# One Strassen level in the down layer of a fused attention and MoE kernel, with one shared pool of four buffers for q, k and v

## Chip, cores, metric

The kernel runs on one core of one Trainium2 chip. The metric is device time in microseconds (us) of one execution. A profile's span is 1.7 to 1.9 us shorter than the time of the same execution. Engine names: PE is TensorE (PEld its weight loads), DVE is VectorE, ACT is ScalarE, POOL is GpSimd, SP is SyncE, which issues stores and transposing DMAs. The granted clock is the mean share of full speed at which PE was clocked. A DMA's landing time runs from its issue to the arrival of its last data.

## The reference, cut to what matters

```python
def _attn_ref(q, k, v, E, F):                     # 8 batches, 8 heads, 1024 tokens, 64 wide
    k_proj = np.einsum('ks,bhsd->bhkd', E, k)     # 1024 keys projected to 64
    v_proj = np.einsum('ks,bhsd->bhkd', F, v)
    scores = (1.0 / np.sqrt(q.shape[-1])) * np.matmul(q, k_proj.transpose(0, 1, 3, 2))
    ...                                           # softmax
    return np.matmul(attn, v_proj)

def _moe_ref(x, w1, w2, w_out):                   # x: 8192 tokens x 512; w1, w2: 512 x 1024
    g = np.maximum(x @ w1, x @ w2)
    return (g @ w_out).astype(np.float32)
```

The code is shortened and its comments are added. The kernel uses max(h1, h2) = relu(h1 - h2) + h2. So the up layer is x (w1 - w2) with a relu, and the down layer multiplies [relu, x] by [w_out, w2 w_out]: an inner dimension of 1024 + 512, or 12 blocks of 128.

## The kernel before

A batch has 1024 tokens in two halves j. In the up layer 8 slots a half run 4 matmuls of 512 columns, and DVE evacuates each bank (a tile of 128 x 512 fp32 in PSUM, into which PE accumulates) with a relu. In the down layer 4 output tiles a half accumulate 12 matmuls of 512 columns, and ACT copies them out. The attention of the next batch is strung between these slots: the projections (`step_kv`), the transpose of k (`step_kpt`), the scores (`step_sc`) and the rest (`step_da`), all in program order on each engine. From batch 2 on a DMA transposes q (`step_qt_dma`).

```python
    kvq = ctx.enter_context(tc.tile_pool(name="kvq", bufs=2))
    proj = ctx.enter_context(tc.tile_pool(name="proj", bufs=2))
    soft = ctx.enter_context(tc.tile_pool(name="soft", bufs=2))
    ...
    gpool = ctx.enter_context(tc.tile_pool(name="gpool", bufs=2))
    hpool = ctx.enter_context(tc.tile_pool(name="hpool", bufs=3))
    opool = ctx.enter_context(tc.tile_pool(name="opool", bufs=4))

    ...

    def mm_bank(dtype=FP32):
        return ps.tile(
            [128, 512 if dtype == FP32 else 1024], dtype, tag="mm", bufs=4, name="mm_ps"
        )

    def att_banks():
        return ps.tile([128, 2, 512], FP32, tag="att", bufs=2, name="att_ps")

    ...

    def alloc_kvq():
        t = {}
        for n in ("k", "v", "q"):
            t[n] = kvq.tile([128, H, NC, D], FP16, tag=n, name=f"{n}_sb")
        return t

    def load(t, n, src, b, h0, h1, c0=0, c1=NC):
        nc.gpsimd.dma_start(
            out=t[n][:, h0:h1, c0:c1, :],
            in_=src[b, h0:h1].rearrange("h (p c) d -> p h c d", c=NC)[:, :, c0:c1, :],
        )

    ...

    def step_qt_dma(t):
        nc.sync.dma_start_transpose(
            out=t["qt"].rearrange("q h (i p) -> q (h i) p", p=128),
            in_=t["q"].rearrange("p h c d -> p (h c d)"),
        )

    ...

    def step_sc(t, p):
        sc_ps = att_banks()
        for o in range(2):
            for e in range(2):
                pos = D * (o ^ e)
                nc.tensor.matmul(
                    out=sc_ps[pos : pos + KP, e, :],
                    lhsT=t["kpt"][o * D : (o + 1) * D, 2 * p + e, :],
                    rhs=t["qt"][o * D : (o + 1) * D, 2 * p + e, :],
                    start=True, stop=True,
                )
        ex = stage.tile([128, 2, HALF], FP16, tag="ex", name="ex_sb")
        t["ex"][p] = ex
        nc.scalar.activation(out=ex, in_=sc_ps, func=ACTF.Exp, scale=scale)

    def step_da(t, p):
        ex = t["ex"].pop(p)
        dn_ps = att_banks()
        at_ps = att_banks()
        for dst, w in ((dn_ps, None), (at_ps, t["vp"])):
            for r in range(2):
                for e in range(2):
                    o = r ^ e
                    rows = slice(r * KP, (r + 1) * KP)
                    nc.tensor.matmul(
                        out=dst[e * D : (e + 1) * D, o, :],
                        lhsT=ones16[rows, 0:D] if w is None else w[rows, 2 * p + e, :],
                        rhs=ex[rows, e, :],
                        start=True, stop=True,
                    )
        ld = soft.tile([128, 2, HALF], FP32, tag="ld", name="ld_sb")
        rec = soft.tile([128, 2, HALF], FP32, tag="rec", name="rec_sb")
        nc.scalar.activation(out=ld, in_=dn_ps, func=ACTF.Ln)
        nc.scalar.activation(out=rec, in_=ld, func=ACTF.Exp, scale=-1.0)

        def finish():
            nc.vector.tensor_tensor(
                out=t["xt"][:, p, :, :], in0=at_ps, in1=rec, op=ALU.mult
            )

        return finish

    ...

    def up_slots(t, j):
        t["gt", j] = gt = gpool.tile([128, NFB, HALF], FP16, tag="gt", name="gt_sb")
        for fb in range(NFB):
            def up(fb=fb):
                h_ps = mm_bank()
                for r in range(NDC):
                    nc.tensor.matmul(
                        out=h_ps,
                        lhsT=wd_sb[:, r, fb * 128 : (fb + 1) * 128],
                        rhs=t["xt"][:, r, :, j * W : (j + 1) * W],
                        start=(r == 0), stop=(r == NDC - 1),
                    )
                nc.vector.tensor_scalar_max(gt[:, fb, :], h_ps, 0.0)
            yield up

    def down_slots(b, t, j):
        for n2 in range(NI):
            o, i = n2 % 2, 2 * j + n2 // 2
            cell = {}
            g0 = (o * 2 + n2 // 2) * 128
            for part in range(3):
                def down(o=o, i=i, g0=g0, cell=cell, part=part):
                    gt = t["gt", j]
                    if part == 0:
                        cell["ps"] = mm_bank()
                    op_ps = cell["ps"]
                    for n in range(4 * part, 4 * part + 4):
                        if n < NFB:
                            lhsT, rhs = gt[:, n, g0 : g0 + 128], wo_sb[:, n, :]
                        else:
                            lhsT = t["xt"][:, n - NFB, o, i * 128 : (i + 1) * 128]
                            rhs = m_sb[:, n - NFB, :]
                        nc.tensor.matmul(
                            out=op_ps, lhsT=lhsT, rhs=rhs,
                            start=(n == 0), stop=(n == NFB + NDC - 1),
                        )
                    if part < 2:
                        return
                    o_sb = opool.tile([128, DM], FP32, tag="o", name="o_sb")
                    nc.scalar.copy(out=o_sb, in_=op_ps)
                    nc.sync.dma_start(
                        out=out.rearrange("(n p c) m -> n p c m", p=128, c=NC)[
                            b, :, 2 * i + o, :
                        ],
                        in_=o_sb,
                    )
                yield down

    ...

    core = {
        7: (step_kv,), 9: (step_kpt,), 13: (step_sc, 0),
        17: (step_da, 0), 19: (step_sc, 1), 23: (step_da, 1), 25: (step_sc, 2),
        29: (step_da, 2), 31: (step_sc, 3), 35: (step_da, 3),
    }
    late = {
        23: (step_kv,), 24: (step_kpt,), 25: (step_qt, 0), 27: (step_qt, 2), 28: (step_sc, 0),
        31: (step_da, 0), 32: (step_qt, 4), 33: (step_sc, 1), 36: (step_da, 1),
        37: (step_qt, 6), 38: (step_sc, 2), 41: (step_da, 2), 43: (step_sc, 3), 45: (step_da, 3),
    }
    by_dma = {1: (step_qt_dma,)}

    for b in range(B):
        nxt = None
        steps = {}
        if b + 1 < B:
            nxt = tiles[b + 1] = alloc_kvq()
            for n, src in (("k", k), ("v", v), ("q", q)):
                load(nxt, n, src, b + 1, 0, H)
            new_attn(nxt)
            steps = {n: [(s[0], nxt, *s[1:])] for n, s in (
                {**core, **by_dma} if b else late).items()}
    ...
```

The softmax here doesn't subtract the row's maximum and nothing guards it: scores larger than these inputs give would overflow.

Of the kernel before, what the change touches and what calls it, by code (L numbers as in the profile page):

```python
# [8 lines left out]
FP32 = mybir.dt.float32  # L9
FP16 = mybir.dt.float16  # L10
LN_EXP_SET = 6
ACTF = mybir.ActivationFunctionType
ALU = mybir.AluOpType
# [3 lines left out]
def kernel(  # L17
# [12 lines left out]
    nc = tc.nc  # L30

    B, H, S, D = q.shape
    KP = E.shape[0]
# [3 lines left out]
    NI = NC // 2  # L37
# [5 lines left out]
    scale = 1.0 / float(D) ** 0.5  # L43

    const = ctx.enter_context(tc.tile_pool(name="const", bufs=1))
    kvq = ctx.enter_context(tc.tile_pool(name="kvq", bufs=2))
    proj = ctx.enter_context(tc.tile_pool(name="proj", bufs=2))
    soft = ctx.enter_context(tc.tile_pool(name="soft", bufs=2))
    qtp = ctx.enter_context(tc.tile_pool(name="qtp", bufs=2))
    stage = ctx.enter_context(tc.tile_pool(name="stage", bufs=4))  # L50
    xpool = ctx.enter_context(tc.tile_pool(name="xpool", bufs=2))
    gpool = ctx.enter_context(tc.tile_pool(name="gpool", bufs=2))
    hpool = ctx.enter_context(tc.tile_pool(name="hpool", bufs=3))
    opool = ctx.enter_context(tc.tile_pool(name="opool", bufs=4))
    ps = ctx.enter_context(tc.tile_pool(name="ps", bufs=1, space=bass.MemoryType.PSUM))

    def mm_bank(dtype=FP32):
        return ps.tile(
            [128, 512 if dtype == FP32 else 1024], dtype, tag="mm", bufs=4, name="mm_ps"
        )  # L60

    def att_banks():
        return ps.tile([128, 2, 512], FP32, tag="att", bufs=2, name="att_ps")
# [12 lines left out]
    )  # L76


    ef_sb = const.tile([KP, 2, S], FP32)
    nc.sync.dma_start(out=ef_sb[:, 0, :], in_=E)  # L80
    nc.sync.dma_start(out=ef_sb[:, 1, :], in_=F)

    def alloc_kvq():
        t = {}
        for n in ("k", "v", "q"):
            t[n] = kvq.tile([128, H, NC, D], FP16, tag=n, name=f"{n}_sb")
        return t

    def load(t, n, src, b, h0, h1, c0=0, c1=NC):
        nc.gpsimd.dma_start(  # L90
# [1 line left out]
            in_=src[b, h0:h1].rearrange("h (p c) d -> p h c d", c=NC)[:, :, c0:c1, :],  # L92
        )

    tiles = {0: alloc_kvq()}
    for h0 in (0, H // 2):
        load(tiles[0], "k", k, 0, h0, h0 + H // 2)
        load(tiles[0], "q", q, 0, h0, h0 + H // 2, 0, NC // 2)
# [3 lines left out]
    load(tiles[0], "v", v, 0, 0, H // 2)  # L102
    load(tiles[0], "v", v, 0, H // 2, H)

    w1_sb = const.tile([128, NDC, DF], FP16)
    w2_sb = const.tile([128, NDC, DF], FP16)
    wo_sb = const.tile([128, NFB, DM], FP16)
    for f0 in range(0, DF, 256):
        if f0 == 256:
# [40 lines left out]
    def new_attn(t):  # L150
        t["kp"] = proj.tile([KP, H, D], FP16, tag="kp", name="kp_sb")
        t["vp"] = proj.tile([128, H, D], FP16, tag="vp", name="vp_sb")
        t["kpt"] = proj.tile([128, H, KP], FP16, tag="kpt", name="kpt_sb")
        t["xt"] = xpool.tile([128, NP2, 2, HALF], FP16, tag="xt", name="xt_sb")
        t["qt"] = qtp.tile([128, H, HALF], FP16, tag="qt", name="qt_sb")
        t["ex"] = {}


    def step_kv(t, h0=0, h1=H, which="kv"):
        kv_ps = mm_bank()  # L160
        n = (h1 - h0) * D
        both = which == "v"
        for c in range(NC):
            for w in which:
                i = "kv".index(w)
                for r in range(2) if both else (i,):
                    nc.tensor.matmul(  # L167
                        out=kv_ps[r * KP : (r + 1) * KP, 0:n],
                        lhsT=eft[:, i, c, :],
                        rhs=t[w][:, h0:h1, c, :],  # L170
                        start=(c == 0), stop=(c == NC - 1),
                    )
        fl = lambda ap: ap[:, h0:h1, :].rearrange("p h d -> p (h d)")
        if "k" in which:
            eng = nc.vector.tensor_copy if which == "k" else nc.scalar.copy
            eng(out=fl(t["kp"]), in_=kv_ps[0:KP, 0:n])  # L176
        if both:
            nc.vector.tensor_copy(out=fl(t["vp"]), in_=kv_ps[:, 0:n])
        elif "v" in which:
            nc.vector.tensor_copy(out=fl(t["vp"][KP:128]), in_=kv_ps[KP:128, 0:n])  # L180
            nc.vector.tensor_copy(out=fl(t["vp"][0:KP]), in_=kv_ps[KP:128, 0:n])


    def step_kpt(t, h0=0, h1=H):
        kpt_ps = mm_bank(FP16)
        for h in range(h0, h1):
            for r in range(2):
                nc.tensor.transpose(  # L188
                    out=kpt_ps[r * D : (r + 1) * D, (h - h0) * KP : (h - h0 + 1) * KP],
                    in_=t["kp"][:, h, :],  # L190
                    identity=ident16[:KP, :KP],
                )
        nc.vector.tensor_copy(
            out=t["kpt"][:, h0:h1, :].rearrange("q h k -> q (h k)"),
            in_=kpt_ps[:, 0 : (h1 - h0) * KP],
        )
# [26 lines left out]
    def step_sc(t, p):  # L223
# [11 lines left out]
        t["ex"][p] = ex  # L235
        nc.scalar.activation(out=ex, in_=sc_ps, func=ACTF.Exp, scale=scale)  # L236

    def step_da(t, p):
        ex = t["ex"].pop(p)
        dn_ps = att_banks()  # L240
        at_ps = att_banks()
# [9 lines left out]
                        start=True, stop=True,  # L251
                    )
        ld = soft.tile([128, 2, HALF], FP32, tag="ld", name="ld_sb")
        rec = soft.tile([128, 2, HALF], FP32, tag="rec", name="rec_sb")
        nc.scalar.activation(out=ld, in_=dn_ps, func=ACTF.Ln)  # L255
        nc.scalar.activation(out=rec, in_=ld, func=ACTF.Exp, scale=-1.0)  # L256

        def finish():
            nc.vector.tensor_tensor(  # L259
# [27 lines left out]
    def two_dn(t, g):  # L287
# [8 lines left out]
                    start=True, stop=True,  # L296
                )
        ld = soft.tile([128, 2, HALF], FP32, tag="ld", name="ld_sb")
        rec = soft.tile([128, 2, HALF], FP32, tag="rec", name="rec_sb")
        nc.scalar.activation(out=ld, in_=dn_ps, func=ACTF.Ln)  # L300
        nc.scalar.activation(out=rec, in_=ld, func=ACTF.Exp, scale=-1.0)
        t["rec", g] = rec

    def two_at(t, g, j):
# [22 lines left out]

    wd_sb = const.tile([128, NDC, DF], FP16)
    m_sb = const.tile([128, NDC, DM], FP16)
    w2t_sb = const.tile([128, NFB, DM], FP16)  # L330


    def up_slots(t, j):
        t["gt", j] = gt = gpool.tile([128, NFB, HALF], FP16, tag="gt", name="gt_sb")
        for fb in range(NFB):
            def up(fb=fb):
                h_ps = mm_bank()
                for r in range(NDC):
                    nc.tensor.matmul(  # L339
                        out=h_ps,  # L340
# [1 line left out]
                        rhs=t["xt"][:, r, :, j * W : (j + 1) * W],  # L342
                        start=(r == 0), stop=(r == NDC - 1),
                    )
                nc.vector.tensor_scalar_max(gt[:, fb, :], h_ps, 0.0)  # L345
            yield up

    def down_slots(b, t, j):
# [53 lines left out]
    def step_m(r):  # L402
# [6 lines left out]
        nc.scalar.copy(out=m_sb[:, r, :], in_=m_ps)  # L409


    t = tiles[0]
    new_attn(t)
    step_kv(t, 0, 4, "k")
    warm(2)
    step_kpt(t, 0, 4)
# [19 lines left out]
    warm(6)  # L436


    core = {
        7: (step_kv,), 9: (step_kpt,), 13: (step_sc, 0),  # L440
        17: (step_da, 0), 19: (step_sc, 1), 23: (step_da, 1), 25: (step_sc, 2),
        29: (step_da, 2), 31: (step_sc, 3), 35: (step_da, 3),
    }
    late = {
        23: (step_kv,), 24: (step_kpt,), 25: (step_qt, 0), 27: (step_qt, 2), 28: (step_sc, 0),
        31: (step_da, 0), 32: (step_qt, 4), 33: (step_sc, 1), 36: (step_da, 1),
        37: (step_qt, 6), 38: (step_sc, 2), 41: (step_da, 2), 43: (step_sc, 3), 45: (step_da, 3),
    }
    by_dma = {1: (step_qt_dma,)}

    for b in range(B):
        nxt = None
        steps = {}
        if b + 1 < B:
            nxt = tiles[b + 1] = alloc_kvq()
            for n, src in (("k", k), ("v", v), ("q", q)):
                load(nxt, n, src, b + 1, 0, H)
            new_attn(nxt)
            steps = {n: [(s[0], nxt, *s[1:])] for n, s in (
                {**core, **by_dma} if b else late).items()}  # L460
        t = tiles[b]
        if b == 0:
            u0, u1 = [*up_slots(t, 0)], [*up_slots(t, 1)]
            wt = [lambda f0=f0: step_w2t(f0) for f0 in range(0, DF, 256)]
            wd = [lambda f0=f0: step_wd(f0) for f0 in range(0, DF, 256)]
            f = lambda s, *a: lambda: s(t, *a)
            seq = [
                u0[0], u0[1], f(step_qt, 0, 4, NI // 2, NI), f(step_qt, 4, 4, NI // 2, NI), lambda: warm(2),
                f(two_sc, 0, 1), f(two_sc, 1, 1), wd[1], u0[2], f(two_dn, 0), u0[3],
                f(two_dn, 1), wd[2], f(two_at, 0, 1), u0[4], u0[5], wt[1], wd[3], f(two_at, 1, 1),  # L470
                wt[2], u0[6], wt[3], u0[7], *u1,
            ]
            base = len(seq) - 20
            seq += [lambda r=r: step_m(r) for r in range(NDC)]
            seq += [*down_slots(b, t, 0), *down_slots(b, t, 1)]
            steps = {n + base: l for n, l in steps.items()}
        else:
            seq = [s for j in range(2) for f in (up_slots(t, j), down_slots(b, t, j)) for s in f]
        pending = []
        for n, slot in enumerate(seq):  # L480
            r = slot()
            for f in pending:
                f()
            pending = [r] if r is not None else []
            for s in steps.get(n, ()):
                r = s[0](*s[1:])
                if r is not None:
                    pending.append(r)
        for f in pending:
            f()  # L490
        del tiles[b]


# [28 lines left out]
```

## Time and profile before

| | before |
|---|---|
| time, median of the first 3 runs (of 4 with a later one) | 370.33 us (370.75) |
| span of the profile | 369.6 us |
| PE, DVE, ACT busy | 97%, 41%, 39% |
| a steady batch (2 to 6) | 41.40 us |
| batch 1 | 43.67 us |
| the down layer's share of a steady batch | 96 matmuls x 0.216 = 20.7 us |

A busy share is an average; what a change is worth is decided by the engine that never waits. Here that is PE. The lines are in the prediction.

### The profile page before, as it was taken

How to read it: one execution, taken by the hardware profiler on the slowest of the kernel's cores; microseconds unless marked ns; L12 is line 12 of the kernel's file. 1: busy time of each engine (PE TensorE's matmuls, PEld its weight loads, DVE VectorE, ACT ScalarE, POOL GpSimd, SP SyncE). 2: the span in 40 equal slices, each digit the busy share in tenths (PEclk: the TensorE clock that was granted, in tenths of full speed). 3: DMA queues.
4: the chain of work that ended last, by engine and by line, in shares of the span. 5: the costliest groups of instructions: out<-in, count | busy, mean ns of one | idle time of the engine just before them, and what ended most of it. 6: DMA issues, size and time to landing. Idle time of an engine off the chain costs nothing.

```text
span 369.6 us, 5092 instructions
## 1 busy us (share of the span) xinstructions
PE 359.0 (97%) x2163; PEld 153.5 (42%) x2163; DVE 149.8 (41%) x206; ACT 144.8 (39%) x177; POOL 31.4 (9%) x43
## 2 busy tenths in 40 slices
PE   8988999999899999999999999999999999999996
PEld 4444444434334443344433444344433444344442
DVE  1377611336053442526163542526163533525140
ACT  2538034670365316460364316560364315550101
POOL 8343010001100020000200020000000000000000
PEclk9999999999999999999999999999999999999999
DMA  8999999999993569927994569926111522020302
GB/s 151 202 196 203 207 207 220 242 243 197 222 234 71 140 104 227 183 85 142 155 243 104 137 99 230 175 87 142 69 48 57 133 67 87 0 87 28 114 28 88
DMA packets 65479, 52.24 MB, mean 141 GB/s; under 512 B 26416, under 2 KB 57136, under 8 KB 65456
## 3 DMA queue, kind: packets, MB, share of 16 engines
q0 software_dynamic: 31312, 28.31, 48.3%
q1 hardware_dynamic: 34144, 23.60, 23.4%
q8 instruction: 17, 0.28, 0.3%
q14 instruction: 6, 0.05, 0.0%
HBM read 57.15 MB, written 16.78 MB: 200 GB/s over the span
## 4 chain that ended last, share of the span: by engine, by line
PE 86%; DMA 8%; DVE 2%; POOL 1%; ACT 1%; issue 1%; DVEq 0%; ACTq 0%; POOLq 0%
PE mm_ps L365 44%; PE mm_ps L339 29%; PE att_ps L247 4%; DMA qt_sb<-q_sb 4%; DMA w_sb<-in_moe_w_dram 4%; PE mm_ps L167 3%; PE att_ps L228 3%; PE mm_ps L405 2%; PE mm_ps L188 1%; PE mm_ps L204 0%; POOL q_sb L90 0%; POOL v_sb L90 0%; DVE wd_sb L383 0%; DVE xt_sb L318 0%; POOL k_sb L90 0%
## 5 line engine op out<-in xcount | busy, mean ns | idle before, releaser
L365 PE MATMUL mm_ps<-wo_sb,gt_sb 128*128 128x512 f16 x512 | 124.0, 380 | 0.0
L339 PE MATMUL mm_ps<-xt_sb,wd_sb 128*128 128x512 f16 x512 | 116.3, 379 | 2.6 <-DVE wd_sb L383 1.1
L345 DVE TENSOR_SCALAR gt_sb<-mm_ps 128x512 f16<-128x512 f32 x128 | 87.4, 690 | 41.1 <-PE mm_ps L339 41.0
L259 DVE TENSOR_TENSOR xt_sb<-att_ps,rec_sb 128x1024 f16<-128x1024 f32 x28 | 34.3, 1225 | 127.3 <-ACT rec_sb L256 127.3
L339 PEld LDWEIGHTS <-wd_sb 128*128 128x128 f16 x512 | 48.3, 98 | 63.9 <-issue 7.3
L365 PEld LDWEIGHTS <-gt_sb 128*128 128x128 f16 x512 | 47.5, 98 | 62.4 <-issue 9.8
L372 ACT COPY o_sb<-mm_ps 128x512 f32<-128x512 f32 x64 | 37.3, 582 | 83.7 <-PE mm_ps L365 75.9
L365 PE MATMUL mm_ps<-m_sb,xt_sb 128*128 128x512 f16 x256 | 65.9, 380 | 0.0
L255 ACT ACTIVATE ld_sb<-att_ps 128x1024 f32<-128x1024 f32 x28 | 28.7, 1024 | 49.0 <-PE att_ps L247 49.0
L365 PEld LDWEIGHTS <-xt_sb 128*128 128x128 f16 x256 | 23.2, 98 | 30.8 <-issue 5.8
L236 ACT ACTIVATE ex_sb<-att_ps 128x1024 f16<-128x1024 f32 x28 | 28.8, 1027 | 5.0 <-PE att_ps L228 4.9
L256 ACT ACTIVATE rec_sb<-ld_sb 128x1024 f32<-128x1024 f32 x28 | 29.6, 1057 | 0.9
L176 ACT CAST kp_sb<-mm_ps 64x512 f16<-64x512 f32 x7 | 4.1, 579 | 51.4 <-PE mm_ps L167 51.4
L90 POOL DMA_DIRECT2D k_sb<-in_k_dram x9 | 7.8, 867 | 156.5 <-PE mm_ps L167 153.2
L167 PE MATMUL mm_ps<-v_sb,eft 128*64 128x512 f16 (+1 forms) x88 | 15.5, 343 | 0.5 <-DMA v_sb<-in_v_dram 0.5
L167 PE MATMUL mm_ps<-k_sb,eft 128*64 128x512 f16 (+1 forms) x72 | 15.5, 358 | 0.3 <-DMA k_sb<-in_k_dram 0.3
L167 PEld LDWEIGHTS <-eft 128*64 128x64 f16 x160 | 8.9, 109 | 10.0 <-issue 3.8
L180 DVE CAST vp_sb<-mm_ps 64x512 f16<-64x512 f32 x7 | 4.9, 694 | 19.4 <-ACT kp_sb L176 19.4
L228 PE MATMUL att_ps<-qt_sb,kpt_sb 64*64 64x512 f16 x112 | 11.5, 400 | 1.2 <-DMA qt_sb<-q_sb 1.2
L125 PE MATMUL mm_ps<-ones 128*128 128x512 f16 x35 | 10.8, 429 | 1.5 <-DVE ones L119 1.5
L247 PE MATMUL att_ps<-ex_sb,ones 64*64 64x512 f16 x112 | 11.5, 400 | 0.0
L247 PE MATMUL att_ps<-ex_sb,vp_sb 64*64 64x512 f16 x112 | 10.8, 376 | 0.0
(47 smaller groups left out, 122.6 us busy)
## 6 DMA issues: line engine op xcount, KB each, us to landing
out_dram<-o_sb SPq DMA_DIRECT2D x64, 256.0 KB, 2.2
k_sb<-in_k_dram POOLq DMA_DIRECT2D x7, 1024.0 KB, 12.3
v_sb<-in_v_dram POOLq DMA_DIRECT2D x7, 1024.0 KB, 17.7
q_sb<-in_q_dram POOLq DMA_DIRECT2D x7, 1024.0 KB, 21.1
w_sb<-in_moe_w_dram POOLq DMA_DIRECT2D x8, 256.0 KB, 14.5
k_sb<-in_k_dram POOLq DMA_DIRECT2D x2, 512.0 KB, 7.8
v_sb<-in_v_dram POOLq DMA_DIRECT2D x2, 512.0 KB, 12.6
wo_sb<-in_moe_w_out_dram POOLq DMA_DIRECT2D x1, 1024.0 KB, 15.7
```

Of the source, the lines that this page charges most:

```text
L125: nc.tensor.matmul(out=w_ps, lhsT=ones16[:, 0:128], rhs=ones16, start=True, stop=True)
L167: nc.tensor.matmul(out=kv_ps[r * KP : (r + 1) * KP, 0:n], lhsT=eft[:, i, c, :], rhs=t[w][:, h0:h1, c, :], start=(c == 0), stop=(c == NC - 1),)
L228: nc.tensor.matmul(out=sc_ps[pos : pos + KP, e, :], lhsT=t["kpt"][o * D : (o + 1) * D, 2 * p + e, :], rhs=t["qt"][o * D : (o + 1) * D, 2 * ...
L236: nc.scalar.activation(out=ex, in_=sc_ps, func=ACTF.Exp, scale=scale)
L247: nc.tensor.matmul(out=dst[e * D : (e + 1) * D, o, :], lhsT=ones16[rows, 0:D] if w is None else w[rows, 2 * p + e, :], rhs=ex[rows, e, :], ...
L255: nc.scalar.activation(out=ld, in_=dn_ps, func=ACTF.Ln)
L256: nc.scalar.activation(out=rec, in_=ld, func=ACTF.Exp, scale=-1.0)
L259: nc.vector.tensor_tensor(out=t["xt"][:, p, :, :], in0=at_ps, in1=rec, op=ALU.mult)
L339: nc.tensor.matmul(out=h_ps, lhsT=wd_sb[:, r, fb * 128 : (fb + 1) * 128], rhs=t["xt"][:, r, :, j * W : (j + 1) * W], start=(r == 0), stop= ...
L345: nc.vector.tensor_scalar_max(gt[:, fb, :], h_ps, 0.0)
L365: nc.tensor.matmul(out=op_ps, lhsT=lhsT, rhs=rhs, start=(n == 0), stop=(n == NFB + NDC - 1),)
L372: nc.scalar.copy(out=o_sb, in_=op_ps)
```

## The change

Its intent: the down layer's product of (tokens x inner) by (inner x outputs) is cut in halves along all three dimensions, and seven block products take the place of eight. This is the form with shared sums (Winograd's): four sums of weight blocks T once, four sums of activation blocks S a batch, all in fp16 on DVE, and seven sums of results, of which four happen by accumulating on in the same bank. The products are 256 columns wide. Batch 0 keeps the plain down layer.

To make room, q, k and v share four buffers instead of six, and the weights' buffers are used again for S. Four relus a batch go to ACT. The last product of a batch runs after the first two up slots of the next. The attention of batch 2 moves ahead, from slot 7 of batch 1 to slot 1 (its scores to slot 4), since batches 3 to 7 now start theirs in the down layer two batches earlier. The core of the diff:

```diff
-    kvq = ctx.enter_context(tc.tile_pool(name="kvq", bufs=2))
+    kvq = ctx.enter_context(tc.tile_pool(name="kvq", bufs=4))
     proj = ctx.enter_context(tc.tile_pool(name="proj", bufs=2))
     soft = ctx.enter_context(tc.tile_pool(name="soft", bufs=2))
     qtp = ctx.enter_context(tc.tile_pool(name="qtp", bufs=2))
-    stage = ctx.enter_context(tc.tile_pool(name="stage", bufs=4))
+    stage = ctx.enter_context(tc.tile_pool(name="stage", bufs=3))
     xpool = ctx.enter_context(tc.tile_pool(name="xpool", bufs=2))
-    gpool = ctx.enter_context(tc.tile_pool(name="gpool", bufs=2))
-    hpool = ctx.enter_context(tc.tile_pool(name="hpool", bufs=3))
-    opool = ctx.enter_context(tc.tile_pool(name="opool", bufs=4))
+    gpool = ctx.enter_context(tc.tile_pool(name="gpool", bufs=1))
+    opool = ctx.enter_context(tc.tile_pool(name="opool", bufs=3))
+    ppool = ctx.enter_context(tc.tile_pool(name="ppool", bufs=4))
...
+    def mm_bank(dtype=FP32, n=None):
+        if n is None:
+            n = turn[0] % 4
+            turn[0] += 1
+        return ps.tile([128, 512 if dtype == FP32 else 1024], dtype, tag=f"mm{n}", name="mm_ps")
...
+    def alloc(t, n):
+        t[n] = kvq.tile([128, H, NC, D], FP16, tag="kvq", name=f"{n}_sb")
+
+    def load_all(t, b, n, src):
+        alloc(t, n)
+        load(t, n, src, b, 0, H)
...
-    def up_slots(t, j):
-        t["gt", j] = gt = gpool.tile([128, NFB, HALF], FP16, tag="gt", name="gt_sb")
+    def up_slots(t, j, banks=None, on_act=()):
+        t["gt", j] = gt = gpool.tile([128, NFB, HALF], FP16, tag=f"gt{j}", name="gt_sb")
...
-                nc.vector.tensor_scalar_max(gt[:, fb, :], h_ps, 0.0)
+                if fb in on_act:
+                    nc.scalar.activation(out=gt[:, fb, :], in_=h_ps, func=ACTF.Relu)
+                else:
+                    nc.vector.tensor_scalar_max(gt[:, fb, :], h_ps, 0.0)
...
+        for out_, x, y in (
+            (T[0], blk(0, 1), blk(0, 0)),
+            (T[1], blk(1, 1), T[0]),
+            (T[2], blk(1, 1), blk(0, 1)),
+            (T[3], blk(1, 0), T[1]),
+        ):
+            nc.vector.tensor_tensor(out=out_, in0=x, in1=y, op=ALU.subtract)
...
+        for i in which:
+            x, y, op = (
+                (blk(1, 0), blk(1, 1), ALU.add),
+                (S[0], blk(0, 0), ALU.subtract),
+                (blk(0, 0), blk(1, 0), ALU.subtract),
+                (blk(0, 1), S[1], ALU.subtract),
+            )[i]
+            for n in range(n1 - n0) if part else (slice(0, n1 - n0),):
+                nc.vector.tensor_tensor(out=S[i][:, n], in0=x[:, n], in1=y[:, n], op=op)
...
+        prods = {
+            1: (A(0, 0), b_block(0, 0)), 2: (A(0, 1), b_block(1, 0)), 3: (Sb(3), b_block(1, 1)),
+            4: (A(1, 1), Tb(3)), 5: (Sb(0), Tb(0)), 6: (Sb(1), Tb(1)), 7: (Sb(2), Tb(2)),
+        }
...
+        def product(g, k, name, first):
+            if first:
+                st[g][name] = mm_bank(n={"X": (0, 2), "Y": (1, 3), "Z": (1, 3)}[name][g])
+            bank = st[g][name]
+            a, w_ = prods[k]
+            for i in range(2):
+                for n in range(NK):
+                    nc.tensor.matmul(
+                        out=bank[:, i * CH : (i + 1) * CH],
+                        lhsT=a(n)[:, g, i * 128 : (i + 1) * 128],
+                        rhs=w_(n),
+                        start=(first and i == 0 and n == 0), stop=(n == NK - 1), skip_group_check=True,
+                    )
+            return bank
...
+        def p1(g):
+            keep(g, "s1", product(g, 1, "X", True))
+
+        def p2(g):
+            bank = product(g, 2, "Y", True)
+            o_tile(g, 0)
+            add(g, 0, 0, bank, st[g]["s1"])
+
+        def p5(g):
+            keep(g, "s5", product(g, 5, "Z", True))
+
+        def p6(g):
+            keep(g, "u2", product(g, 6, "X", False))
+
+        def p3(g):
+            add(g, 0, 1, product(g, 3, "Z", False), st[g]["u2"])
+            store(g, 0)
+
+        def p7(g):
+            keep(g, "u3", product(g, 7, "X", False))
+            o_tile(g, 1)
+            add(g, 1, 1, st[g]["u3"], st[g]["s5"])
+
+        def p4(g):
+            bank = product(g, 4, "X", False)
+            nc.scalar.copy(out=cols(st[g]["o", 1], 0), in_=two(bank))
+            store(g, 1)
+
+        order = (p1, 0), (p2, 0), (p1, 1), (p2, 1), (p5, 0), (p6, 0), (p3, 0), (p7, 0), (p5, 1), \
+            (p4, 0), (p6, 1), (p3, 1), (p7, 1), (p4, 1)
+        return [lambda f=f, g=g: f(g) for f, g in order]
...
+        banks = None if b == 1 else (0, 1, 3, 2)
+        seq = [*up_slots(t, 0, banks, (2, 6)), *up_slots(t, 1, banks, (2, 6))]
+        seq += down_steps(b, t)
+        own = [((b, n), x) for n, x in enumerate(seq)]
+        if b > 1:
+            last = slots.pop()
+            own[2:2] = [last]
+        slots += own
...
+        elif b == 2:
+            at_slot(0, 43, new_attn, t)
+            at_slot(0, 43, step_qt_dma, t)
+            plan = "kv 1, kpt 2, sc0 4, da0 6, sc1 8, da1 10, sc2 12, da2 14, sc3 16, da3 19"
         else:
...
+            at_slot(b - 2, 7, new_attn, t)
+            at_slot(b - 2, 7, step_qt_dma, t)
+            plan = "kv -25, kpt -27, sc0 -28, da0 2, sc1 4, da1 7, sc2 10, da2 13, sc3 16, da3 19"
...
+            if name == "kv":
+                at_slot(w_, n, step_kv, t, 0, H, "kv", 1 if b > 2 else None)
+                at_slot(w_, n, loads, b + 1, "v", "q", *(() if b == 1 else ("k",)))
...
+    at_slot(0, 21, step_t, 0)
+    at_slot(0, 22, step_t, 1)
+    for b in range(1, B):
+        for i in range(4):
+            at_slot(b, 4 + i, step_s, tiles[b], (i,), 1)
+        at_slot(b, 12, step_s, tiles[b], (2,), 0)
+        at_slot(b, 15, step_s, tiles[b], (0, 1, 3), 0)
```

## The prediction

> **What bounds the kernel now.** I read the page's first two parts, then stretches of one batch, then the PE timeline, then the waits, and last DVE and the DMA queue of SP, because a change that takes work from PE has to be paid on the others. The page says that PE is the bound: 97% busy, at the full clock, with every other compute engine near 40%.
>
> ```profile
> PE 359.0 (97%) x2163; PEld 153.5 (42%) x2163; DVE 149.8 (41%) x206; ACT 144.8 (39%) x177; POOL 31.4 (9%) x43
> ...
> PEclk9999999999999999999999999999999999999999
> ...
> L365 PE MATMUL mm_ps<-wo_sb,gt_sb 128*128 128x512 f16 x512 | 124.0, 380 | 0.0
> ...
> L345 DVE TENSOR_SCALAR gt_sb<-mm_ps 128x512 f16<-128x512 f32 x128 | 87.4, 690 | 41.1 <-PE mm_ps L339 41.0
> L259 DVE TENSOR_TENSOR xt_sb<-att_ps,rec_sb 128x1024 f16<-128x1024 f32 x28 | 34.3, 1225 | 127.3 <-ACT rec_sb L256 127.3
> ```
>
> Line 365 is the down layer, 345 the relu that evacuates the up layer, 259 the attention product. Busy time of pipelined matmuls overlaps, so I took the pace from stretches. One batch in the steady state is 41.40 us with PE never idle; the last batch is 34.6 us of matmuls and then a tail. Columns of the stretches: its length, then PE, PEld, DVE, ACT, POOL busy.
>
> ```profile
> 80.60:124.27 43.67, 41.69 (x242) 17.05 (x240) 18.70 (x24) 17.46 (x22) 2.63 (x3) 1.00 0.94 174
> 124.27:165.67 41.40, 41.40 (x242) 16.99 (x241) 17.47 (x23) 17.09 (x21) 2.63 (x3) 1.00 0.76 153
> 165.67:207.07 41.40, 41.40 (x242) 17.03 (x241) 17.47 (x23) 17.09 (x21) 2.63 (x3) 1.00 0.78 153
> 331.40:369.60 38.20, 34.54 (x161) 15.48 (x158) 11.07 (x16) 5.27 (x9) 0.00 (x0) 1.00 0.18 66
> ```
>
> The reader sees that batches repeat exactly (nothing but PE sets 41.40), and that batch 1 took 2.27 us more. That is two waits: 0.78 us at its start for the last attention product, and 1.20 us at its first scores for the transposed q. In the chain of waits 48 down matmuls of 512 columns take 10.36 us, 0.216 us each, so the down layer is 96 x 0.216 = 20.7 us of the 41.4.
>
> The pace of narrower matmuls is the whole question, since the new products have 256 columns and reload weights at each one. Two early stretches of the PE timeline answer it, and two of DVE's show its pace without gaps (start, length, ..., count):
>
> ```profile
> 8.22 1.03 PE L167 MATMUL mm_ps<-k_sb,eft 128*64 128x256 f16 x8 [0.34 <-DMA k_sb<-in_k_dram]
> ...
> 25.29 1.06 PE L204 MATMUL mm_ps<-ident,q_sb 128*128 128x128 f16 x16
> ```
> ```profile
> 27.39 0.69 DVE L383 TENSOR_TENSOR wd_sb<-w_sb 128x1024 f16<-128x1024 f16 x1
> ...
> 194.21 1.88 DVE L345 TENSOR_SCALAR gt_sb<-mm_ps 128x512 f16<-128x512 f32 x3
> ```
>
> Eight matmuls of 256 columns: (1.03 - 0.276 for the last one's own duration) / 7 = 108 ns a piece. Sixteen transposes of 128 columns, each with its own 128x128 weight load: (1.06 - 0.22) / 15 = 56 ns. So a full weight load per 128 columns does not slow PE, and one per 256 columns certainly should not. On DVE three relus in a row take 1.88 us: a relu that follows another costs 0.595 us, not 0.69; I call this the queued pace.
>
> **What the Trainium skill says.** "TensorE: Matmul & The Clock Gate", section Back-to-back issue gap, gives N/2.4 + 2.5 ns: 109 ns at 256 columns and 216 at 512; the trace agrees (108, 216). The same section puts streams of load and matmul at about 81 ns for 128 columns; this trace has 56, and the measurement decides. "VectorE: DVE Perf Modes", section The perf-mode tier table, caps tensor_tensor at two elements a cycle for 16-bit operands in SBUF and at one for fp32 or PSUM. The trace agrees: 1024 fp16 elements in 0.69 us, 1024 from PSUM and fp32 in 1.225. "DMA: Bandwidth & Descriptors", section Queues, rings and completion order, says that each DMA engine takes turns between queues. The trace agrees: the transposing DMA of q landed in 15.4 us in batch 1, amid loads, and in 6.8 us (median) otherwise. "TensorEngine Tiling (Array Packing)", section Key Properties, says that a change of tiling mode drains TensorE; here each interruption by attention costs about 0.1 us (8 matmuls between two of them take 1.83 us, not 1.73). Their number does not change.
>
> **The change part by part.**
> 1. *Products.* Seven products x 2 halves o x 2 row blocks x 6 = 168 matmuls of 256 columns, at 0.1092 (the formula above) 18.35 us, for 20.73. That is 2.38 a batch, and in seven batches **-16.7 us**, all on PE's path.
> 2. *Schedule of batch 1.* Its last attention step moves two slots ahead (1.7 us), which covers the 0.78 us wait, and the 1.20 us wait changes its place (5). **-2.0.**
> 3. *DVE.* Added per batch: eight pieces of 512 fp16 (0.42 each, as the 512-element copy of kpt), four of 2048 fp16 ((2048/2 + 150 cycles of overhead, from the 0.69 us of 1024) / 0.96 = 1.22) and six fp32 sums of 512 (0.69, as the other 512-element fp32 products). That is 3.4 + 4.9 + 4.1 = 12.4 us. Four relus go to ACT: -2.8. So 17.5 + 9.6 = 27 of some 39 us: not the bound over a batch. But it bunches: while the up layer runs (16 x 0.864 us, with 3 attention steps and 2 score steps 16.8, plus 1.3 for the previous batch's last product, which now sits there) DVE gets one sum, 12 relus, 3 attention products and five groups of sums, 17.2 us at full durations and 15 at the queued pace. I walked both queues in order, with PE held when a bank's relu four slots back is not done. At full durations the relus fall 3.5 us behind and PE waits 0.6 + 1.0 us at slots 12 and 13. At the queued pace the lag stays under 3 us and PE waits 0.35. After the up layer come three sums of 2048 (3.4 us), which the first four products (5.2 us) cover. I take 0.5 a batch with what ACT adds (below), six batches: **+3.0.**
> 4. *ACT.* Eight copies of fp32 banks become ten (+1.2 us) and four relus come (+2.3): 20.6 of 39. Its two-microsecond pair for the last attention step can delay one saved product by 0.15 us (counted in 3).
> 5. *q of batch 2.* Its scores move from slot 13 of batch 1 to slot 4. The DMA that transposes q still starts after batch 0's last store, at 82.0. PE gets to the scores at 80.7 + 5 x 0.864 + 1.85 (kv) + 0.5 (kpt) + breaks = 87.8. At 6.8 us the transpose lands at 88.8; the loads of v and q that now start at some 86 delay it. I take 90: **+2.** With the 15.4 us of before it would be +9.6, but v and q of batch 3, which filled the queue then, are now loaded later.
> 6. *Four shared buffers.* Loads keep their order and start once the batch before has been projected. That leaves 15 us before q is to be transposed and 40 before v is needed, against 17.7 and 12.3 us landing for the second and first of three loads: hidden.
> 7. *Tail.* The last store is 512 KB instead of 256 KB: **+1.** The sums over the weights (4.5 us on DVE, once) lie in batch 0's down layer, where DVE is mostly idle.
>
> Sum: 369.6 - 16.7 - 2.0 + 3.0 + 2.0 + 1.0 = 356.9 of span. The time measured is 0.7 over the span before (370.33 against 369.6), so 357.6.
>
> **Rivals.** (a) *DVE paces the up layer.* For it: 17.2 us of work in 18, in strict order, with attention products that block the relus behind them. Against: the queued pace. It would cost 1.7 x 6 = 10 us instead of 3: 365. (b) *The transposed q of batch 2 is late* by the whole 15.4 us: 365 as well; both together 372, no gain at all. (c) *256-column products don't hold 109 ns* since a load and its matmul share the array: at 123 ns the saving is zero and the time about 374. The transposes speak against it, but each of them runs in a burst of at most 16. (d) *The products wait for their banks*, since each of them accumulates on the one before and its copy has only one product's time (1.31 us) to finish; at 0.3 us for half of the 14 products it is +2 a batch, 371. For: ACT's copy is 0.58 and an exponential of 1.03 us may stand in front. Against: few exponentials lie in those slots.
>
> **Range and chances.** Most of what is uncertain makes it slower; full hiding of 3 and 5 gives 353. So 352.5 to 364.5. Within 2% means above 362.9; (a) or (b) alone would do it, and I give the two, with (c) and (d), some 17 in 100. More than 2% slower would need (c).
>
> **What would show it.** The steady batch should last 39.4 us (41.40 - 2.38 + 0.4). Products of 256 columns: a run of 12 in 1.3 + 0.1 us. PE's idle time released by DVE relus should be under 0.5 us a batch; more is rival (a). One wait of some 2 us for the transposed q near 88 us; none later. DVE's busy time in a steady batch 27 us, less what overlaps. Wrong would be a product pace over 115 ns, or steady batches over 40.5 us.

## The result, and the profile after

Ratios are the mean time of one kernel's fast runs over that of the other's in the same rounds, so they are not quite the ratio of the medians quoted.

| | before | after |
|---|---|---|
| time, median | 370.75 us (4 runs) | 364.94 us (363.97 to 365.88, 4 runs) |
| ratio | | 0.984 (0.981 to 0.988) |
| span of the profile | 369.6 us | 362.2 us |
| steady batch | 41.40 us | 39.36 us |
| batch 1 | 43.67 us | 48.74 us |
| mean granted clock of PE | 1.00 | 0.988 |

So the kernel is 1.6% faster, where 3.4% was predicted (357.6 us after 370.33). The profile before is of the slowest of its four executions and the one after of the fastest, so the spans differ by 7.4 us and the medians by 5.8. First the page after the change: the busy lines, the clock in 40 slices of 9 us, and the groups of the products, the kept copies, the adds and the large sums.

```profile
PE 345.6 (95%) x2667; PEld 203.5 (56%) x2667; DVE 209.9 (58%) x312; ACT 169.3 (47%) x219; POOL 31.3 (9%) x43
...
PEclk9999999999699999999999999999999999999998
...
L520 ACT COPY p_sb<-mm_ps 128x512 f32<-128x512 f32 x56 | 32.7, 583 | 65.2 <-PE mm_ps L510 60.1
L510 PE MATMUL mm_ps<-T_sb,big 128*128 128x256 f16 x504 | 59.7, 273 | 1.2 <-DVE o_sb L530 1.1
...
L530 DVE TENSOR_TENSOR o_sb<-mm_ps,p_sb 128x512 f32<-128x512 f32 x28 | 18.7, 687 | 22.5 <-PE mm_ps L510 22.4
...
L491 DVE TENSOR_TENSOR big<-gt_sb 128x2048 f16<-128x2048 f16 x14 | 17.1, 1218 | 0.6
```

The clock has a 6 in the eleventh slice, 90.6 to 99.6 us; before it had none. Next the stretches, in the columns of the prediction, for the start of batch 1, its slow middle, batch 1 as a whole, two steady batches and the last batch:

```profile
80.45:90.00 9.55, 6.75 (x53) 2.75 (x50) 5.15 (x9) 1.76 (x3) 1.75 (x2) 1.00 0.92 178
90.00:108.00 18.00, 14.88 (x81) 5.13 (x82) 10.13 (x17) 9.87 (x12) 0.87 (x1) 0.81 1.24 219
...
80.45:129.19 48.74, 42.74 (x338) 24.36 (x336) 26.83 (x39) 21.00 (x28) 5.24 (x6) 0.93 0.91 167
129.19:168.55 39.36, 39.13 (x313) 24.10 (x314) 25.43 (x37) 20.60 (x28) 2.62 (x3) 1.00 0.88 160
168.55:207.91 39.36, 39.13 (x313) 24.15 (x314) 25.43 (x37) 20.60 (x28) 2.62 (x3) 1.00 0.84 163
...
323.20:362.20 39.00, 33.78 (x245) 23.68 (x242) 19.89 (x31) 9.41 (x16) 0.00 (x0) 0.97 0.22 82
```

Steady batches gained what they should (39.4 was predicted), with PE busy in all but 0.23 us of each. The loss is in batch 1: PE is idle for 6 us of it, and in its middle the granted clock is 0.81. (By its content batch 1 should last 1.4 us more than a steady batch: it has a second projection, transpose of k and scores, +2.7, and passes its last product on, -1.3. It lasts 9.4 more; the other 8.0 are an estimate of the loss. Run 1 gives it directly: 48.74 against 40.96 us, 7.8.) PE's timeline there shows both effects:

```profile
92.92 0.64 PE L239 MATMUL att_ps<-qt_sb,kpt_sb 64*64 64x512 f16 x4 [5.72 <-DMA qt_sb<-q_sb]
93.50 3.60 PE L355 MATMUL mm_ps<-xt_sb,wd_sb 128*128 128x512 f16 x8
```

PE waits 5.72 us for the transposed q. Then the eight up matmuls behind the scores take 3.53 us in the chain of waits, where eight take 1.83 elsewhere: half the clock (0.50 granted from 93 to 97 us), so some 2 us lost. In the kernel before this wait was 1.2 us, by its list of waits (total, times, longest):

```profile
PE att_ps L228 <- DMA qt_sb<-q_sb: 1.2, 1, 1.2
```

Last, a steady batch and the end, in the chain of waits, which follows the work that ended last back to what released it (start, length, what):

```profile
149.00 4.05 PE mm_ps L510 x36
153.09 0.69 DVE o_sb L530
153.83 8.02 PE mm_ps L510 x72
...
188.36 4.05 PE mm_ps L510 x36
...
338.33 17.20 PE mm_ps L510 x156
355.54 0.59 ACT p_sb L520
356.18 1.48 PE mm_ps L510 x12
357.69 0.58 ACT o_sb L566
```

The steady batch is the distance of the first and the fourth line, 39.36 us; in it product 5 (with the 72 matmuls) starts behind an add on DVE, which holds its bank. At the end, the last product accumulates on a bank that ACT must first copy. In other batches two up slots lie between the two; in the last batch nothing does, and PE waits 0.67 us.

### The profile page after: what moved, and what is told of

It is laid out like the page before. It is cut to its first block, busy times and chain, and to the rows that moved or that the text cites. A ratio compares the mean times of both kernels' runs of the same rounds, so it can differ in the third digit from the quotient of the medians.

```text
span 362.2 us, 6214 instructions
## 1 busy us (share of the span) xinstructions
PE 345.6 (95%) x2667; PEld 203.5 (56%) x2667; DVE 209.9 (58%) x312; ACT 169.3 (47%) x219; POOL 31.3 (9%) x43
## 4 chain that ended last, share of the span: by engine, by line
PE 85%; DMA 7%; DVE 3%; ACT 1%; POOL 1%; issue 1%; DVEq 0%; POOLq 0%
PE mm_ps L510 36%; PE mm_ps L355 30%; PE mm_ps L384 6%; DMA v_sb<-in_v_dram 4%; PE mm_ps L178 3%; DMA qt_sb<-q_sb 3%; PE att_ps L263 3%; PE att_ps L239 3%; PE mm_ps L424 2%; DVE o_sb L530 1%; PE mm_ps L199 1%; ACT big L417 1%; DVE gt_sb L364 1%; PE mm_ps L215 0%; POOL q_sb L100 0%
## 5 line engine op out<-in xcount | busy, mean ns | idle before, releaser
L364 DVE TENSOR_SCALAR gt_sb<-mm_ps 128x512 f16<-128x512 f32 x100 | 67.3, 685 | 33.8 <-PE mm_ps L355 33.7
L355 PEld LDWEIGHTS <-wd_sb 128*128 128x128 f16 x512 | 47.0, 98 | 64.7 <-issue 15.4
L510 PEld LDWEIGHTS <-big 128*128 128x128 f16 x672 | 64.9, 98 | 13.3 <-issue 3.7
L520 ACT COPY p_sb<-mm_ps 128x512 f32<-128x512 f32 x56 | 32.7, 583 | 65.2 <-PE mm_ps L510 60.1
L510 PE MATMUL mm_ps<-T_sb,big 128*128 128x256 f16 x504 | 59.7, 273 | 1.2 <-DVE o_sb L530 1.1
L275 DVE TENSOR_TENSOR xt_sb<-att_ps,ld_sb 128x1024 f16<-128x1024 f32 x28 | 34.2, 1222 | 27.1 <-ACT ld_sb L271 27.1
L247 ACT ACTIVATE ex_sb<-att_ps 128x1024 f16<-128x1024 f32 x28 | 28.7, 1025 | 12.2 <-PE att_ps L239 11.3
L510 PE MATMUL mm_ps<-wo_sb,gt_sb 128*128 128x256 f16 x224 | 33.7, 273 | 0.2 <-DVE gt_sb L364 0.2
L530 DVE TENSOR_TENSOR o_sb<-mm_ps,p_sb 128x512 f32<-128x512 f32 x28 | 18.7, 687 | 22.5 <-PE mm_ps L510 22.4
L271 ACT ACTIVATE ld_sb<-ld_sb 128x1024 f32<-128x1024 f32 x28 | 29.6, 1057 | 0.9
L510 PE MATMUL mm_ps<-m_sb,xt_sb 128*128 128x256 f16 x112 | 21.4, 273 | 0.0
L491 DVE TENSOR_TENSOR big<-gt_sb 128x2048 f16<-128x2048 f16 x14 | 17.1, 1218 | 0.6
```

Of the source, the lines that this page charges most:

```text
L271: nc.scalar.activation(out=ld, in_=ld, func=ACTF.Exp, scale=-1.0)
L275: nc.vector.tensor_tensor(out=t["xt"][:, p, :, :], in0=at_ps, in1=rec, op=ALU.mult)
L355: nc.tensor.matmul(out=h_ps, lhsT=wd_sb[:, r, fb * 128 : (fb + 1) * 128], rhs=t["xt"][:, r, :, j * W : (j + 1) * W], start=(r == 0), stop= ...
L491: nc.vector.tensor_tensor(out=S[i][:, n], in0=x[:, n], in1=y[:, n], op=op)
L510: nc.tensor.matmul(out=bank[:, i * CH : (i + 1) * CH], lhsT=a(n)[:, g, i * 128 : (i + 1) * 128], rhs=w_(n), start=(first and i == 0 and n ...
L520: nc.scalar.copy(out=x, in_=bank)
```

## The experiments

The theory after the result: the products gain what was computed, and the missing gain is batch 1's wait for q, whose length is the transposing DMA's sharing of the DMA engines with the loads of batch 3, and whose idle time also halves PE's clock; a small rest is at the end. The chief rival: DVE paces the changed kernel, and the wait for q hides it. Runs 1 to 4 shared a chip and the runs of the kernel before (370.50 us, median of 11), runs 5 to 7 another set (371.05 us, 7).

### 1. The transpose earlier

```diff
-            at_slot(0, 43, new_attn, t)
-            at_slot(0, 43, step_qt_dma, t)
+            at_slot(0, 35, new_attn, t)
+            at_slot(0, 35, step_qt_dma, t)
```

> The DMA that transposes q of batch 2 starts at slot 35 of batch 0 instead of slot 43 (q landed at 71.2 us in the changed kernel, the scores come at 87). Theory (the lost time is batch 1's 5.7 us wait for the transposed q, and about 2.1 us of matmuls at half clock behind it): the transpose lands by 85, the wait is gone, the granted clock is 1.00, batch 1 lasts 41 to 42 us instead of 48.7, span 354.4, time 356.2, ratio to before 0.961. Rival (VectorE paces batch 1, and the wait only hid its lag; two projections and all sums lie there): the wait goes but PE then waits 3 us or more for relus, time 359 to 361.

Measured: 356.70 us (356.57 to 357.40, 4 runs), ratio 0.962 (0.960 to 0.964), span 354.8, clock 0.999. The transpose started at 72.4 and landed 12.2 us later. PE's timeline at the same scores:

```profile
87.53 0.41 PE L239 MATMUL att_ps<-qt_sb,kpt_sb 64*64 64x512 f16 x4
87.87 1.90 PE L355 MATMUL mm_ps<-xt_sb,wd_sb 128*128 128x512 f16 x8
```

No wait is shown at the scores, and the eight matmuls run at the full clock. Batch 1 lasts 40.96 us (80.85 to 121.81) instead of 48.74, so all of the 7.8 us came back; the span fell by 7.4, since batch 1 began 0.4 us later. So DVE was not behind the wait: the rival falls. The move is two numbers; the transfer took even longer than before, but nothing was waiting.

### 2. The wait filled with dummy work

```diff
+            at_slot(1, 4, warm, 24)
             plan = "kv 1, kpt 2, sc0 4, da0 6, sc1 8, da1 10, sc2 12, da2 14, sc3 16, da3 19"
```

> 24 dummy matmuls (5.2 us) are put in front of batch 2's first scores, so PE works through its wait. Theory (the idle time of 5.7 us itself lowers PE's clock, which costs 2 us more than the wait): the transpose lands at the same 92.9, granted clock 1.00 instead of 0.988, the eight up matmuls behind the scores take 1.8 instead of 3.5 us, span 360.2, time 362.9. Rival (the low clock in the record costs nothing, matmuls there wait for something else): time unchanged at 364.9.

Measured: 362.31 us (361.88 to 362.92, 5 runs), ratio 0.977 (0.975 to 0.979), span 360.1, clock 0.997.

```profile
92.78 0.41 PE L239 MATMUL att_ps<-qt_sb,kpt_sb 64*64 64x512 f16 x4 [0.53 <-DMA qt_sb<-q_sb]
93.13 1.90 PE L355 MATMUL mm_ps<-xt_sb,wd_sb 128*128 128x512 f16 x8
```

The transposed q comes at the same moment (92.8), yet the kernel is 2.6 us faster in the medians, 2.1 in the spans and 2.0 in batch 1 (46.73 us): PE that works through its wait keeps its clock. So the 7.8 us of run 1 are some 5.7 of waiting and 2 of clock.

### 3. The loads held back

```diff
+    hold_sb = const.tile([128, 1], FP16)
 ...
     def loads(b, *names):
+        if b == 3:
+            nc.gpsimd.tensor_copy(out=hold_sb, in_=tiles[1]["gt", 0][:, 3, 0:1])
 ...
-                at_slot(w_, n, loads, b + 1, "v", "q", *(() if b == 1 else ("k",)))
+                at_slot(w_, 3 if b == 2 else n, loads, b + 1, "v", "q", *(() if b == 1 else ("k",)))
```

> The loads of v and q of batch 3 (and k of 4) wait for the relu of slot 3 of batch 1, by a one-element copy on GpSimd, so they start some 2.5 us later, at about 87.5 instead of 84.3. Theory (the transpose lands late because those loads share the DMA engines with it): it lands near 89 instead of 92.8, PE waits 1 to 2 us instead of 5.7, no low clock, time 359. Rival (the transpose takes 11 us whatever else runs, from its own 4500 packets): it lands at 92.8 and the time is 364.9.

Measured: the profiled run took 359.46 us with the transpose landing after 8.4 us instead of 11.2, a wait of 3.0 us (1 to 2 expected) and the full clock. The landing times of this one DMA, in the kernel before, the changed kernel and this run:

```profile
qt_sb<-q_sb SPq DMA_TRANSPOSE x1, 15.4
...
qt_sb<-q_sb SPq DMA_TRANSPOSE x1, 11.2
...
qt_sb<-q_sb SPq DMA_TRANSPOSE x1, 8.4
```

So the sharing is real: holding the loads gave back 2.8 us of landing, less than the 3.8 expected. The packets show where it bites. In the changed kernel all but some 250 of the transpose's 4,140 packets (the ones under 512 B) had moved by 88.0 us, and all but 32 by 89.0; these came between 91.0 and 92.5, behind some 290 packets of the loads. So the loads held up the last few packets, not the bulk. In this run, with the loads issued from 87.9 on, all but 43 had moved by 88.0, and all but 2 by 88.5. Why those two came only after 89.0, behind half a microsecond without any packet, stays open. The median of the 6 runs is 361.51 (359.46 to 362.65), ratio 0.975 (0.972 to 0.977), worse than the expected 359: the other five runs have granted clocks of 0.989 to 0.993 and 361.4 to 362.7 us. A wait of 3.0 us thus left the clock alone in one execution. In the other five it may not have, but that is not shown: their profiles weren't kept, so their waits are not known, and a lower clock alone doesn't tell, since one execution of run 1 had 0.992 too and the kernel before 0.993 to 0.995 in several.

```profile
90.35 0.41 PE L239 MATMUL att_ps<-qt_sb,kpt_sb 64*64 64x512 f16 x4 [3.00 <-DMA qt_sb<-q_sb]
90.69 1.90 PE L355 MATMUL mm_ps<-xt_sb,wd_sb 128*128 128x512 f16 x8
```

### 4. The order and the last store of the last batch

```diff
             (p4, 0), (p6, 1), (p3, 1), (p7, 1), (p4, 1)
+        if b == B - 1:
+            order = (*order[:9], *order[10:13], order[9], order[13])
 ...
+            if b == B - 1 and g == 1:
+                store(g, 1, CH, DM)
 ...
-            store(g, 1)
+            store(g, 1, 0, CH if b == B - 1 and g == 1 else DM)
```

The first store comes after product 7's add, when half of the output columns are done.

> In the last batch alone the product 4 of half 0 is put between the products 7 and 4 of half 1, and the last store is split, so that only 256 KB are left for the end. Theory: the 0.67 us wait of the last product for the copy of its bank goes, and the end after the last matmul shrinks from 4.6 to 4 us: span 360.9, time 363.6, ratio to before 0.981. Rival (the tail is fixed by the last DMA's latency): only the 0.67 us goes, 364.3.

Measured: 363.51 us (363.35 to 364.40, 4 runs), ratio 0.981 (0.978 to 0.983), span 361.7. In the chain of waits the last 168 matmuls of products now run as one piece:

```profile
339.08 18.50 PE mm_ps L510 x168
357.61 0.59 ACT o_sb L568
```

18.50 us, where the changed kernel has 17.20 + 0.65 + 1.48 = 19.3. From the end of the last copy to the end of the span it is 361.7 - 358.2 = 3.5 us, where it was 362.2 - 358.27 = 3.9. So the wait went as expected, and the end shrank by 0.4 of the 0.6 expected. The span fell by only 0.5 because batch 1 of this execution began 0.9 us later (81.35 against 80.45); its wait for q was no longer (5.6 us). The ranges of the two kernels' times overlap, so the chain shows this gain, and the times alone don't; that the median met the forecast of 363.6 is in part chance.

### 5. The sums of activations made tiny

```diff
+        width = slice(0, W if t is tiles[1] else 2)
-                nc.vector.tensor_tensor(out=S[i][:, n], in0=x[:, n], in1=y[:, n], op=op)
+                nc.vector.tensor_tensor(
+                    out=S[i][:, n][..., width], in0=x[:, n][..., width], in1=y[:, n][..., width], op=op)
```

The S buffers are taken once here and shared by all batches.

> A wrong result on purpose: from batch 2 on each sum of blocks writes 2 columns per block row instead of 256, so VectorE is freed of nearly all of the sums' 8.3 us a batch while PE's work and the order of everything stays. Theory (the sums cost PE 0.2 to 0.3 us a batch, by the wait of product 5 for VectorE's add, and nothing else): steady batch 39.1 instead of 39.36, batch 1 unchanged with its wait, time 363.2. Rival (the gap between 41.40 - 2.38 = 39.02 and 39.36 belongs to PE, such as more mode changes or product starts): steady batch still 39.3.

Measured: 362.76 us (362.55 to 363.14, 4 runs), ratio 0.979, span 361.1; the result is wrong, as meant. In the chain of waits the same 36 products start every 39.02 us, exactly 41.40 - 2.38:

```profile
149.71 4.04 PE mm_ps L515 x36
...
188.73 4.04 PE mm_ps L515 x36
...
227.74 4.04 PE mm_ps L515 x36
```

So PE's part of the change is the computed saving with no remainder, and all that the sums cost a batch is 0.34 us.

### 6. All relus back on DVE

```diff
-        seq = [*up_slots(t, 0, banks, (2, 6)), *up_slots(t, 1, banks, (2, 6))]
+        seq = [*up_slots(t, 0, banks, ()), *up_slots(t, 1, banks, ())]
```

> All relus back on VectorE (the change gave four of sixteen a batch to ScalarE). Theory (VectorE is close to pacing the up layer: 15 us at its queued pace in 18, and 4 more relus of 0.6 fill it): PE waits 1 to 2 us a batch for relus, steady batch 40.4 to 41.4, time 371 to 377, the gain of the change gone. Rival (there is room for them): steady batch up to 39.6, time 365 to 366.5.

Measured: 369.87 us (369.37 to 370.39, 4 runs), ratio 0.998 (0.995 to 1.001), span 367.9. The steady batch is 40.18 us (the chain's 36 products start at 190.39 and 230.56), a little under the range expected, and the gain of the change is gone, as expected. PE's waits in this run:

```profile
PE att_ps L239 <- DMA qt_sb<-q_sb: 6.0, 1, 6.0
PE mm_ps L510 <- DVE o_sb L530: 3.9, 7, 0.8
PE mm_ps L355 <- DVE gt_sb L364: 1.8, 5, 0.4
```

Here DVE does make PE wait: for relus (0.4 us in each of five batches) and for product 5's add (up to 0.8). In the changed kernel the first of these is nil and the second at most 0.2. So the theory had the size about right and the place only in part: it expected 1 to 2 us a batch for relus, and the larger part came at the add. DVE is busy for 70% of such a batch (27.59 of 39.36 us in a stretch of that length), yet four relus more cost 0.82 us a batch. The likely reason, not tested alone, is that they come where the relus, the attention products and the sums are crowded.

### 7. A better version

Runs 1 and 4 together, and the third large sum moved behind the add that product 5 waits for:

```diff
-        at_slot(b, 15, step_s, tiles[b], (0, 1, 3), 0)
+        at_slot(b, 15, step_s, tiles[b], (0, 1), 0)
+        at_slot(b, 17, step_s, tiles[b], (3,), 0)
```

> The early transpose and the last batch's order together, and the third large sum (for product 3) moved from slot 15 to slot 17, behind the add that product 5 waits for. Theory: the 0.23 us wait of product 5 in each batch goes, steady batch 39.1; with the early transpose 354.8 and the end (-0.67 and -0.4) the span is 352.4, time 354.1, ratio to before 0.956. Rival (moving the sum makes product 3 wait instead): steady batch 39.36 or more, time 355.5 or more.

Measured: 353.80 us (353.11 to 354.16, 4 runs), ratio 0.954 (0.952 to 0.956), span 352.2; the result is correct. The steady batch is 39.07 us (the 36 products start at 141.80 and 180.87), PE is busy in all of it, and the wait for the add is not in PE's list any more. This version beats both kernels.

```profile
PE 344.4 (98%) x2667; PEld 203.2 (58%) x2667; DVE 209.3 (59%) x312; ACT 169.5 (48%) x219; POOL 31.3 (9%) x43
...
PEclk9999999999999999999999999999999999999999
```

## Why the prediction was right or wrong

The measured 364.94 us lie 7.3 above the predicted 357.6 and 0.4 above the range; the gain was 5.8 us by the medians, where 12.7 was forecast. The step that failed is step 5, the landing of the transposed q of batch 2, and with it a cost that no step had, that of PE's clock. By the prediction's own terms, in us of span (the measured ones are from the profile after, and from runs 1, 2 and 5):

| term | predicted | measured |
|---|---|---|
| 1 products | -16.7 | -16.7 (7 x 2.38, run 5) |
| 2 batch 1's two old waits | -2.0 | -2.0 |
| 3, 4 DVE and ACT | +3.0 | +2.0 (6 x 0.34) |
| 5 wait for q of batch 2 | +2.0 | +5.7 |
| clock after that wait | none | +2.1 (runs 1 and 2) |
| 7 end: last store | +1.0 | +1.0 |
| end: last product's wait | none | +0.7 |
| sum | -12.7 | -7.2 (-7.4 by the spans) |

*Right.* The pace of the products (1), against rival (c): a run of 12 takes 1.31 us, 0.109 each, so a 128x128 weight load each 256 columns hides, and the trace's early transposes had shown as much. The estimate of the large sums on DVE held too (1.22 us). The queued pace of DVE fits against rival (a): PE waits for no relu in a steady batch, where the walk at full durations had 1.6 us of such waits. The walk had the place wrong, though: the 0.23 us that PE does wait is for product 5's bank, held by an add that stands behind three large sums (runs 5 and 7), which is nearer to rival (d). The shared buffers (6) cost nothing that shows, though no run tests them alone: PE has no wait for a load behind batch 0.

*Wrong: step 5*, "At 6.8 us the transpose lands at 88.8; the loads of v and q that now start at some 86 delay it. I take 90". It landed at 92.8. The loads started at 84.3 and 85.2, not at 86, and slowed the transpose from 6.7 us alone to 11.2. The trace of before had offered a value for such company: 15.4 us amid loads, 6.8 without. I set it between the two, close to the lower end, and called the upper one rival (b). Run 3 shows 2.8 us of these 4.5 to be the loads' doing (the other 1.7 stay open), run 1 shows the cost.

*Missing: the clock.* Rival (b) and step 5 counted a wait as its own length. The Trainium skill, "TensorE: Matmul & The Clock Gate", section What's actually happening, says that PE's clock falls to half after an idle window of about 3.4 us, and that the window runs free of what the kernel does. The trace agrees: behind 5.72 us of idling eight matmuls took 3.53 instead of 1.83 us, and 3.0 us (run 3) left it alone in the one profiled execution. A predicted wait has to be held against that length: at the 2 us I took, there would by that page have been no such cost, and at the 5.7 that came it added over a third (2.1 us).

*Missing: the last batch.* The chain of copies and products has a gap of two up slots that exist only when another batch follows (run 4).

*A slip of 1 us in the time.* The 0.7 us added to the span compared the median of three runs with the span of another execution. That profiled execution took 371.33 us for its 369.6, so 1.7 was to be added. The rest of the 7.3 is 5.3 us of span and about 1 us by which the profiled run is the fastest of its four.

*Smaller slips*, which changed nothing: GpSimd is busy for 9%, not near 40; the steady batch of 39.4 us takes 0.4 for DVE where step 3 takes 0.5; and rival (c) at 123 ns gives 374 us, 1% slower than before, so that more than 2% would need a still slower pace.

Of the terms that erred, all but that of DVE erred to the same side. The range ended at 364.5, just under the 365 given for (a) or (b) alone; what came was over half of (b) (5.7 of 9.6 us) with a cost of clock, an end and a slip on top.

## What to carry to other kernels

When work is taken from the bounding engine, check each transfer that the new schedule asks for earlier, and take its duration from the trace under the traffic that it will meet, not alone; then ask whether the wait that comes out is long enough to lower PE's clock, since here a wait of 5.7 us cost 7.8. Fewer products paid here in full (run 5), with the sums on an engine that was idle more than half of the time, but what counts is how the sums bunch: moving four relus of sixteen was worth the whole gain (run 6), and moving one sum behind an add removed PE's last wait in a steady batch (run 7).

## What the Trainium skill lacked or had wrong

- "TensorE: Matmul & The Clock Gate", section Back-to-back issue gap: about 81 ns per matmul for streams of load and matmul at 128 columns, and 131 at 512. Here 16 transposes of 128 columns with a load each ran at 56 ns, 48 matmuls of 512 at 216 ns (10.36 us, before), and 168 products of 256 at 110 ns (18.50 us, run 4).
- The same page, section What's actually happening, gives the idle window but no chance for a wait near its length. In run 3 the profiled execution had a wait of 3.0 us and a clock of 1.00; the other five had 0.989 to 0.993, with waits that are not known.
- "DMA: Bandwidth & Descriptors", section DMA Transpose (X-bar), has no duration under load. A transpose of 1 MB landed in 6.7 us alone, in 8.4 with the loads held off until most of it had moved (run 3), in 11.2 with two loads of 1 MB issued during it, in 15.4 in the kernel before.
- "VectorE: DVE Perf Modes", section The TRN2 errata, gives durations (691 ns for an fp32 tensor_tensor of 512; 687 here for the adds), from which the pace of a row of independent ops can't be told: three relus took 1.88 us, 0.60 from start to start where one lasts 0.69. Rival (a) turned on that difference.
